# Loading the first x rows of a SiLU layer's forward and backward pass as four 128-row tiles, and starting the first matmuls on 384 rows

## The chip, the cores and the metric

The kernel runs on one core of one Trainium2 chip. The metric is the device time of one execution in microseconds (us), as a median over runs. The profile's span (first to last recorded instruction) is 1.7 to 2.4 us shorter than that time. Moments such as "5.25 us" count from the start of the span. PE is TensorE, PEld its weight loads, DVE VectorE, ACT ScalarE, SP SyncE.

## The reference

```python
B, S, D, F = 1, 2048, 640, 1536          # all bfloat16
def forward(x, w1, w2):
    h = einsum("bsd,df->bsf", x, w1)
    return einsum("bsf,fd->bsd", silu(h), w2)
# outputs: forward(x, w1, w2) and the gradients for x, w1, w2, given grad_out
```

That is six matrix products of 2048 x 640 x 1536.

## The kernel before

The 2048 rows are worked in four chunks of 512. Each chunk needs x transposed (`xT`, D on the partitions). Chunks 1 to 3 use a DMA transpose. Chunk 0 loads x as it lies and transposes it on TensorE, 20 blocks of 128x128. Ahead of that stand 36 matmuls on zeros ("warm-ups"): the first matmuls of this program run at half pace, 107 ns from start to start against 56 ns later (shown below), and the warm-ups are there to take up that time.

```python
warm = cpool.tile([P, P], dt_in, name="warm")
nc.vector.memset(warm[:], 0.0)
...                                            # activation table is loaded here
for i in range(NWARM):                         # NWARM = 36
    nc.tensor.matmul(wp[:, 0:P], lhsT=warm[:], rhs=warm[:], start=True, stop=True)
...
def pe_xT(c, halves):                          # called as pe_xT(0, 1)
    xT = xpool.tile([P, DT, SC], dt_in, name="xT")
    ...
        for dt_ in range(DT):                  # 5 blocks of D
            tp = ps_h.tile([P, nst, P], dt_in, name="tp", tag="hp")
            for j in range(nst):               # 4 blocks of rows
                nc.tensor.transpose(tp[:, j, :], x_nat[:, st, dt_*P:(dt_+1)*P], ident[:])
            ...                                # copy to xT, DVE and ACT in turn
# one queue (SP), in this order: 640 KB of x, two pieces of w1 (320 KB each), the rest
nc.sync.dma_start(out=x_nat[:, 0:STC, :], in_=x_v[:, 0:STC, :])
nc.sync.dma_start(out=w1_nat[:, :, 0:FH], in_=w1_v[:, :, 0:FH])       # FH = 256 columns
nc.sync.dma_start(out=w1_nat[:, :, FH:FC], in_=w1_v[:, :, FH:FC])
...
def h_group(ft, xT, aT, ghT):                  # 12 of these make the h stage of a chunk
    hp = ps_h.tile([P, SC], FP32, name="hp")
    for dt_ in range(DT):
        nc.tensor.matmul(hp[:], lhsT=w1_nat[:, dt_, ft*P:(ft+1)*P], rhs=xT[:, dt_, :],
                         start=(dt_ == 0), stop=(dt_ == DT - 1))
    ...                                        # silu and its derivative on ACT and DVE
```

In chunk 0 the h stage (60 matmuls) is followed by the output stage (60 matmuls with w2). The moment at which the output stage's first matmul starts tells how long the head and the h stage took together.

Of the kernel before, what the change touches and what calls it, by code (L numbers as in the profile page):

```python
# [8 lines left out]
ACT = mybir.ActivationFunctionType  # L9
ALU = mybir.AluOpType  # L10
FP32 = mybir.dt.float32
# [4 lines left out]
def kernel(  # L16
# [11 lines left out]
    nc = tc.nc  # L28
    P = 128
# [8 lines left out]
    ST, DT, FT = S // P, D // P, F // P  # L38
    SC = 512
    NCH = S // SC  # L40
    STC = SC // P
    DH = D // 2
    FC = 512
    NFC = F // FC
    LAG = 2
    NWARM = 36
    dt_in = x.dtype

    dram = ctx.enter_context(tc.tile_pool(name="dram", bufs=1, space=bass.MemoryType.DRAM))
# [2 lines left out]
    ps_h = ctx.enter_context(tc.tile_pool(name="ps_h", bufs=8, space=bass.MemoryType.PSUM))  # L52
# [8 lines left out]
    x_nat = natpool.tile([P, ST, D], dt_in, name="x_nat")  # L61

    w1_v = w1.rearrange("(dt p) f -> p dt f", p=P)
    w2_v = w2.rearrange("(ft p) d -> p ft d", p=P)
    x_v = x2.rearrange("(st p) d -> p st d", p=P)
# [17 lines left out]
    with ExitStack() as mctx:  # L83
        cpool = mctx.enter_context(tc.tile_pool(name="cpool", bufs=1))
        wpool = mctx.enter_context(tc.tile_pool(name="wpool", bufs=1))
        xpool = mctx.enter_context(tc.tile_pool(name="xpool", bufs=2))
# [1 line left out]
        tpool = mctx.enter_context(tc.tile_pool(name="tpool", bufs=3))  # L88
        opool = mctx.enter_context(tc.tile_pool(name="opool", bufs=2))

        warm = cpool.tile([P, P], dt_in, name="warm")
        nc.vector.memset(warm[:], 0.0)  # L92
        warm_a = cpool.tile([P, 1], FP32, name="warm_a")
        nc.scalar.activation(warm_a[:], warm[:, 0:1], ACT.Silu)
        wp = ps_h.tile([P, SC], FP32, name="wp", tag="hp")
        for i in range(NWARM):
            nc.tensor.matmul(wp[:, 0:P], lhsT=warm[:], rhs=warm[:], start=True, stop=True)  # L97

        ident = cpool.tile([P, P], dt_in, name="ident")
        make_identity(nc, ident[:])  # L100

        w1_nat = w1pool.tile([P, DT, F], dt_in, name="w1_nat", tag="w1a")
# [4 lines left out]
        def load_xT(c):  # L107
            xT = xpool.tile([P, DT, SC], dt_in, name="xT")
            nc.sync.dma_start_transpose(out=xT[:], in_=x2[c * SC:(c + 1) * SC, :])
            return xT  # L110

        def load_goT(c):
            goT = xpool.tile([P, DT, SC], dt_in, name="goT")
            nc.sync.dma_start_transpose(out=goT[:], in_=go2[c * SC:(c + 1) * SC, :])
            return goT

        def pe_xT(c, halves):
            xT = xpool.tile([P, DT, SC], dt_in, name="xT")
            nst = STC // halves
            for hh in range(halves):  # L120
                for dt_ in range(DT):
                    tp = ps_h.tile([P, nst, P], dt_in, name="tp", tag="hp")
                    for j in range(nst):
                        st = c * STC + hh * nst + j
                        nc.tensor.transpose(tp[:, j, :], x_nat[:, st, dt_ * P:(dt_ + 1) * P], ident[:])  # L125
                    dst = xT[:, dt_, hh * nst * P:(hh + 1) * nst * P]
                    if dt_ % 2 == 0:
                        nc.vector.tensor_copy(out=dst, in_=tp[:].rearrange("p j q -> p (j q)"))
                    else:
                        nc.scalar.copy(out=dst, in_=tp[:].rearrange("p j q -> p (j q)"))  # L130
            return xT

        FH = FC // 2
        nc.sync.dma_start(out=x_nat[:, 0:STC, :], in_=x_v[:, 0:STC, :])
        nc.sync.dma_start(out=w1_nat[:, :, 0:FH], in_=w1_v[:, :, 0:FH])
        nc.sync.dma_start(out=w1_nat[:, :, FH:FC], in_=w1_v[:, :, FH:FC])
        for fc in range(1, NFC):
            nc.sync.dma_start(out=w1_nat[:, :, fc * FC:(fc + 1) * FC], in_=w1_v[:, :, fc * FC:(fc + 1) * FC])
        for hf in range(2):
            nc.sync.dma_start(out=w2_nat[:, :, hf * DH:(hf + 1) * DH], in_=w2_v[:, :, hf * DH:(hf + 1) * DH])  # L140
        goT_next = load_goT(0)
# [1 line left out]
            nc.sync.dma_start_transpose(out=w2T[:, :, fc * FC:(fc + 1) * FC], in_=w2[fc * FC:(fc + 1) * FC, :])  # L143
        nc.sync.dma_start_transpose(out=w1T[:], in_=w1[:, :])

        xT_next = pe_xT(0, 1)

        def h_group(ft, xT, aT, ghT):
            hp = ps_h.tile([P, SC], FP32, name="hp")
            for dt_ in range(DT):  # L150
                nc.tensor.matmul(  # L151
                    hp[:],
                    lhsT=w1_nat[:, dt_, ft * P:(ft + 1) * P],
                    rhs=xT[:, dt_, :],
                    start=(dt_ == 0),
                    stop=(dt_ == DT - 1),
                )
            nc.scalar.activation(aT[:, ft, :], hp[:], ACT.Silu)  # L158
            t = tpool.tile([P, SC], FP32, name="t")
            nc.scalar.activation(t[:], hp[:], ACT.Tanh, scale=0.5)  # L160
            v = tpool.tile([P, SC], dt_in, name="v")
            nc.vector.tensor_scalar(out=v[:], in0=t[:], scalar1=-0.5, scalar2=0.5, op0=ALU.mult, op1=ALU.add)  # L162
            nc.vector.scalar_tensor_tensor(  # L163
                out=ghT[:, ft, :], in0=aT[:, ft, :], scalar=1.0, in1=v[:], op0=ALU.subtract, op1=ALU.mult
            )

        def g_group(ft, goT, ghT):
            gp = ps_h.tile([P, SC], FP32, name="hp")
            for dt_ in range(DT):
                nc.tensor.matmul(  # L170
                    gp[:],
                    lhsT=w2T[:, dt_, ft * P:(ft + 1) * P],
                    rhs=goT[:, dt_, :],
                    start=(dt_ == 0),
                    stop=(dt_ == DT - 1),
                )
            nc.vector.scalar_tensor_tensor(  # L177
                out=ghT[:, ft, :], in0=ghT[:, ft, :], scalar=1.0, in1=gp[:], op0=ALU.add, op1=ALU.mult
            )
# [21 lines left out]
        for c in range(NCH):  # L201
            xT, goT = xT_next, goT_next
            aT = apool.tile([P, FT, SC], dt_in, name="aT")
            ghT = apool.tile([P, FT, SC], dt_in, name="ghT")

            if c + 1 < NCH:
                xT_next = load_xT(c + 1)
                goT_next = load_goT(c + 1)
            if c == 1:
                for j in range(0, ST, STC):  # L210
                    nc.sync.dma_start(out=go_nat[:, j:j + STC, :], in_=go_v[:, j:j + STC, :])
            if c == 2:
                for j in range(STC, ST, STC):
                    nc.sync.dma_start(out=x_nat[:, j:j + STC, :], in_=x_v[:, j:j + STC, :])

            if c == 0:
                for ft in range(FT):
                    h_group(ft, xT, aT, ghT)
                nc.sync.dma_start(
                    out=aT_scr[:, c * SC:(c + 1) * SC].rearrange("(ft p) s -> p ft s", p=P), in_=aT[:]  # L220
                )
                sd_phase(c, w2_nat, aT, oT_scr)
                for ft in range(FT):
                    g_group(ft, goT, ghT)
                nc.sync.dma_start(
                    out=ghT_scr[:, c * SC:(c + 1) * SC].rearrange("(ft p) s -> p ft s", p=P), in_=ghT[:]
                )
                sd_phase(c, w1T, ghT, gxT_scr)
                continue

            for i in range(FT + LAG):
                if i < FT:
                    h_group(i, xT, aT, ghT)
                if i >= LAG:
                    g_group(i - LAG, goT, ghT)

            store_rows(c - 1, opool)
            nc.sync.dma_start(
                out=aT_scr[:, c * SC:(c + 1) * SC].rearrange("(ft p) s -> p ft s", p=P), in_=aT[:]
            )  # L240
            nc.sync.dma_start(
                out=ghT_scr[:, c * SC:(c + 1) * SC].rearrange("(ft p) s -> p ft s", p=P), in_=ghT[:]
            )
            if c == NCH - 1:
                load_a_blk(0, w1pool, "w1a")

            sd_phase(c, w2_nat, aT, oT_scr)
            sd_phase(c, w1T, ghT, gxT_scr)

    with ExitStack() as fctx:  # L250
# [19 lines left out]
        for fc in range(NFC):  # L270
            a_blk = a_blks[fc]
            g2T = fpool.tile([P, DT, FC], dt_in, name="g2T")
            for dt_ in range(DT):
                gp = ps_h.tile([P, FC], FP32, name="hp")
                for st in range(ST):
                    nc.tensor.matmul(  # L276
                        gp[:],
                        lhsT=go_nat[:, st, dt_ * P:(dt_ + 1) * P],
                        rhs=a_blk[:, st, :],
                        start=(st == 0),  # L280
                        stop=(st == ST - 1),
# [15 lines left out]
        for fc in range(NFC):  # L297
            gh_blk = gh_blks[fc]
            for dt_ in range(DT):
                if dt_ == DT // 2:  # L300
                    store_gw2(fc)
                if fc == NFC - 1 and dt_ == DT - 1:
                    for k, (lo, hi) in enumerate(((0, FC - P), (FC - P, FC))):
                        gp = ps_h.tile([P, FC], FP32, name="hp")
                        for st in range(ST):
                            nc.tensor.matmul(  # L306
                                gp[:, lo:hi],
                                lhsT=x_nat[:, st, dt_ * P:(dt_ + 1) * P],
                                rhs=gh_blk[:, st, lo:hi],
                                start=(st == 0),  # L310
                                stop=(st == ST - 1),
# [4 lines left out]
                        else:  # L316
                            nc.vector.tensor_copy(out=g1[:, lo:hi], in_=gp[:, lo:hi])  # L317
                        nc.sync.dma_start(
                            out=gw1_v[:, dt_, fc * FC + lo:fc * FC + hi], in_=g1[:, lo:hi]
# [3 lines left out]
                for st in range(ST):  # L323
                    nc.tensor.matmul(  # L324
                        gp[:],
                        lhsT=x_nat[:, st, dt_ * P:(dt_ + 1) * P],
                        rhs=gh_blk[:, st, :],
                        start=(st == 0),
                        stop=(st == ST - 1),
# [38 lines left out]
```

## Time and profile before

321.74 us (three runs). The busy table of the page gives this row for TensorE and its weight loads, busy us, share of the span and instructions:

```profile
PE 316.2 (99%) x1512; PEld 146.7 (46%) x1512; DVE 101.9 (32%) x179; ACT 78.3 (24%) x140; POOL 0.7 (0%) x6
```

TensorE bounds the kernel. The chain of waits, in order of time (start us, duration us, what the end waited for), for the first 20 us:

```profile
0.74 4.51 DMA x_nat<-in_x_dram
5.25 0.05 issue
5.30 1.29 PE tp L125 x20
6.59 12.95 PE hp L151 x60
```

The reader is to see a head of 6.6 us, then one stream: 60 matmuls in 12.95 us, 216 ns each, and so on to 317.5 us without a gap. The timeline of TensorE shows the warm-ups, the transposes and h:

```profile
0.99 4.02 PE L97 MATMUL wp<-warm 128*128 128x128 bf16 x36 [0.99 <-DVE warm L92]
5.30 1.29 PE L125 MATMUL tp<-ident,x_nat 128*128 128x128 bf16 x20 [0.28 <-DMA x_nat<-in_x_dram]
```

36 warm-ups start 107 ns apart. The 20 transposes have the same size but take 64 ns each, 56 ns from start to start: between the last warm-up and 5.30 us the clock has been released to full pace. (The clock column of the windows below prints 1.00 throughout and does not show this release; it is read from the spacing of equal instructions.) Windows of half a microsecond show how x arrives. The columns are the window, its length, busy us (and instructions) of PE, PEld, DVE, ACT and POOL, the granted clock, the DMA share and GB/s; only the last two matter here:

```profile
1.75:2.25 0.50, 0.50 (x8) 0.50 (x7) 0.00 (x0) 0.47 (x2) 0.00 (x0) 1.00 0.74 115
2.25:2.75 0.50, 0.50 (x7) 0.50 (x6) 0.00 (x0) 0.00 (x0) 0.00 (x0) 1.00 0.65 125
2.75:3.25 0.50, 0.50 (x8) 0.50 (x6) 0.00 (x0) 0.00 (x0) 0.00 (x0) 1.00 0.83 261
```

### The profile page before, as it was taken

Reading aid. Unit: us, or ns where it says so; the run is one execution under the profiler, and the core shown is the slowest. Engines: PE = TensorE matmul, PEld = TensorE weight load, DVE = VectorE, ACT = ScalarE, POOL = GpSimd, SP = SyncE. Lnnn points to the kernel's source line nnn. Section 1 sums busy time; section 2 is a strip of 40 time slices with the busy share of each in tenths; the row PEclk is TensorE's granted clock in tenths of the full one; section 3 lists DMA queues with packets and bytes.
Section 4 is the critical chain, followed back from the end, with each engine's and each line's share of the span. In section 5 each row is a group of like instructions: output and inputs, shape, how many; then the busy total and the mean of one; then the engine's idle time right before and its main releaser. Section 6 shows DMA issues by size and latency. Waiting matters only on the chain.

```text
span 320.1 us, 3590 instructions
## 1 busy us (share of the span) xinstructions
PE 316.2 (99%) x1512; PEld 146.7 (46%) x1512; DVE 101.9 (32%) x179; ACT 78.3 (24%) x140; POOL 0.7 (0%) x6
## 2 busy tenths in 40 slices
PE   8999999999999999999999999999999999999996
PEld 7444444444444444444444444444444444444443
DVE  1871551477510087710147751000000100001001
ACT  3960001555201255401154520110100001001100
POOL 0000000000000000000000000000000000000000
DMA  8999999999999855291635079809999999994111
GB/s 232 314 194 190 252 222 274 341 263 309 262 286 296 227 180 151 69 324 63 175 109 146 2 247 269 224 16 301 260 241 242 269 209 342 238 293 166 52 37 47
DMA packets 149200, 66.69 MB, mean 208 GB/s; under 512 B 112576, under 2 KB 149184, under 8 KB 149184
## 3 DMA queue, kind: packets, MB, share of 16 engines
q1 hardware_dynamic: 149184, 66.46, 81.8%
q8 instruction: 12, 0.20, 0.3%
q14 instruction: 4, 0.03, 0.0%
HBM read 9.18 MB, written 28.97 MB: 119 GB/s over the span
## 4 chain that ended last, share of the span: by engine, by line
PE 98%; DMA 1%; DVE 0%; issue 0%; DVEq 0%
PE hp L186 32%; PE hp L151 16%; PE hp L276 16%; PE hp L170 16%; PE hp L324 15%; DMA x_nat<-in_x_dram 1%; PE hp L306 1%; PE tp L125 0%; DVE g_2364 L317 0%; DVEq L317 0%
## 5 line engine op out<-in xcount | busy, mean ns | idle before, releaser
L151 PE MATMUL hp<-xT,w_nat 128*128 128x512 bf16 x240 | 56.9, 379 | 0.0
L170 PE MATMUL hp<-goT,w2T 128*128 128x512 bf16 x240 | 56.9, 379 | 0.0
L186 PE MATMUL hp<-aT,w_nat 128*128 128x512 bf16 x240 | 52.5, 379 | 0.0
L186 PE MATMUL hp<-ghT,w1T 128*128 128x512 bf16 x240 | 52.5, 379 | 0.0
L276 PE MATMUL hp<-a_blk,go_nat 128*128 128x512 bf16 x240 | 52.0, 379 | 0.0
L324 PE MATMUL hp<-gh_blk,x_nat 128*128 128x512 bf16 x224 | 48.5, 379 | 0.0
L194 ACT ACTIVATE oT<-hp 128x512 bf16<-128x512 f32 x24 | 14.3, 597 | 110.0 <-PE hp L186 110.0
L186 PEld LDWEIGHTS <-w_nat 128*128 128x128 bf16 x240 | 23.5, 98 | 28.3
L170 PEld LDWEIGHTS <-w2T 128*128 128x128 bf16 x240 | 23.5, 98 | 28.3
L276 PEld LDWEIGHTS <-go_nat 128*128 128x128 bf16 x240 | 23.5, 98 | 28.3
L186 PEld LDWEIGHTS <-w1T 128*128 128x128 bf16 x240 | 23.4, 98 | 28.4
L158 ACT ACTIVATE aT<-hp 128x512 bf16<-128x512 f32 x48 | 28.7, 598 | 31.1 <-PE hp L151 31.1
L151 PEld LDWEIGHTS <-w_nat 128*128 128x128 bf16 x240 | 23.4, 98 | 28.1
L196 DVE CAST oT<-hp 128x512 bf16<-128x512 f32 x16 | 11.1, 692 | 78.0 <-PE hp L186 78.0
L177 DVE SCALAR_TENSOR_TENSOR ghT<-ghT,hp 128x512 bf16<-128x512 bf16 x48 | 32.5, 683 | 7.3 <-PE hp L170 7.3
L324 PEld LDWEIGHTS <-x_nat 128*128 128x128 bf16 x224 | 21.9, 98 | 26.4
L163 DVE SCALAR_TENSOR_TENSOR ghT<-aT,v 128x512 bf16<-128x512 bf16 x48 | 33.0, 688 | 0.6
L162 DVE TENSOR_SCALAR v<-t 128x512 bf16<-128x512 f32 x48 | 20.5, 427 | 28.5 <-ACT t L160 28.5
L160 ACT ACTIVATE t<-hp 128x512 f32<-128x512 f32 x48 | 28.4, 591 | 0.0
L286 DVE CAST g2T<-hp 128x512 bf16<-128x512 f32 x7 | 4.8, 692 | 46.1 <-PE hp L276 46.1
L284 ACT ACTIVATE g2T<-hp 128x512 bf16<-128x512 f32 x8 | 4.8, 598 | 47.0 <-PE hp L276 47.0
L97 PE MATMUL wp<-warm 128*128 128x128 bf16 x36 | 4.0, 313 | 1.0 <-DVE warm L92 1.0
(32 smaller groups left out, 27.0 us busy)
## 6 DMA issues: line engine op xcount, KB each, us to landing
aT_scr<-aT SPq DMA_DIRECT2D x4, 1536.0 KB, 6.2
ghT_scr<-ghT SPq DMA_DIRECT2D x4, 1536.0 KB, 10.1
out_dram<-o_sb SPq DMA_DIRECT2D x8, 640.0 KB, 3.4
x_nat<-in_x_dram SPq DMA_DIRECT2D x4, 640.0 KB, 4.7
oT_scr<-oT SPq DMA_DIRECT2D x4, 640.0 KB, 4.3
go_nat<-in_grad_out_dram SPq DMA_DIRECT2D x4, 640.0 KB, 7.1
gxT_scr<-oT SPq DMA_DIRECT2D x4, 640.0 KB, 4.7
w_nat<-in_w_dram SPq DMA_DIRECT2D x2, 960.0 KB, 11.3
```

What stands on the lines that cost most here:

```text
L151: nc.tensor.matmul(hp[:], lhsT=w1_nat[:, dt_, ft * P:(ft + 1) * P], rhs=xT[:, dt_, :], start=(dt_ == 0), stop=(dt_ == DT - 1),)
L158: nc.scalar.activation(aT[:, ft, :], hp[:], ACT.Silu)
L160: nc.scalar.activation(t[:], hp[:], ACT.Tanh, scale=0.5)
L162: nc.vector.tensor_scalar(out=v[:], in0=t[:], scalar1=-0.5, scalar2=0.5, op0=ALU.mult, op1=ALU.add)
L163: nc.vector.scalar_tensor_tensor(out=ghT[:, ft, :], in0=aT[:, ft, :], scalar=1.0, in1=v[:], op0=ALU.subtract, op1=ALU.mult)
L170: nc.tensor.matmul(gp[:], lhsT=w2T[:, dt_, ft * P:(ft + 1) * P], rhs=goT[:, dt_, :], start=(dt_ == 0), stop=(dt_ == DT - 1),)
L177: nc.vector.scalar_tensor_tensor(out=ghT[:, ft, :], in0=ghT[:, ft, :], scalar=1.0, in1=gp[:], op0=ALU.add, op1=ALU.mult)
L186: nc.tensor.matmul(op_[:], lhsT=w_all[:, ft, dt_ * P:(dt_ + 1) * P], rhs=rhs_all[:, ft, :], start=(ft == 0), stop=(ft == FT - 1),)
L194: nc.scalar.activation(oT[:, dt_, :], op_[:], ACT.Copy)
L196: nc.vector.tensor_copy(out=oT[:, dt_, :], in_=op_[:])
L276: nc.tensor.matmul(gp[:], lhsT=go_nat[:, st, dt_ * P:(dt_ + 1) * P], rhs=a_blk[:, st, :], start=(st == 0), stop=(st == ST - 1),)
L324: nc.tensor.matmul(gp[:], lhsT=x_nat[:, st, dt_ * P:(dt_ + 1) * P], rhs=gh_blk[:, st, :], start=(st == 0), stop=(st == ST - 1),)
```

## The change

The intent is to start h earlier: load x as four tiles of 128 rows on two queues, transpose each as it lands, and run h's first two column groups on the first 384 rows, with tile 3 transposed between them. Warm-ups drop from 36 to 26 and start earlier, on a constant that exists anyway; four filler matmuls cover the last copy.

```diff
-    NWARM = 36
+    NWARM = 26
+    NFILL = 4
-        warm = cpool.tile([P, P], dt_in, name="warm")
-        nc.vector.memset(warm[:], 0.0)
+        warm = nc.const_aps.tensor(1.0, (P, P), dt_in)
 ...
-        nc.sync.dma_start(out=x_nat[:, 0:STC, :], in_=x_v[:, 0:STC, :])
-        nc.sync.dma_start(out=w1_nat[:, :, 0:FH], in_=w1_v[:, :, 0:FH])
-        nc.sync.dma_start(out=w1_nat[:, :, FH:FC], in_=w1_v[:, :, FH:FC])
+        load_x_tile(nc.sync, 0)
+        load_x_tile(nc.scalar, 1)
+        load_x_tile(nc.scalar, 2)
+        load_w1(0, FH)
+        load_x_tile(nc.sync, 3)
+        load_w1(FH, FC)
 ...                                  # the activation table is loaded behind these issues
-        xT_next = pe_xT(0, 1)
+        def pe_x_tile(xT, st):       # 3 blocks -> one DVE copy, 2 blocks -> one ACT copy
+            ...
+        for st in range(STC - 1):
+            pe_x_tile(xT_next, st)
+        for i in range(NFILL):
+            nc.tensor.matmul(wp[:, 0:P], lhsT=ident[:], rhs=x_nat[:, STC-2, 0:P], ...)
 ...
             if c == 0:
-                for ft in range(FT):
+                for ft in range(2):                    # XL = 384
+                    h_mm(hp, ft, xT, 0, XL)
+                    if ft == 0:
+                        pe_x_tile(xT, STC - 1)
+                for ft in range(2):
+                    h_mm(hps[ft], ft, xT, XL, SC)
+                    h_group(ft, xT, aT, ghT, hps[ft])
+                for ft in range(2, FT):
                     h_group(ft, xT, aT, ghT)
```

More of the change, by code (lines that the diff above doesn't have):

```diff
@@ L89 @@
         opool = mctx.enter_context(tc.tile_pool(name="opool", bufs=2))
-        warm = cpool.tile([P, P], dt_in, name="warm")
-        nc.vector.memset(warm[:], 0.0)
+        warm = nc.const_aps.tensor(1.0, (P, P), dt_in)
         warm_a = cpool.tile([P, 1], FP32, name="warm_a")
-        nc.scalar.activation(warm_a[:], warm[:, 0:1], ACT.Silu)
         wp = ps_h.tile([P, SC], FP32, name="wp", tag="hp")
         for i in range(NWARM):
-            nc.tensor.matmul(wp[:, 0:P], lhsT=warm[:], rhs=warm[:], start=True, stop=True)
+            nc.tensor.matmul(wp[:, 0:P], lhsT=warm, rhs=warm, start=True, stop=True)
         ident = cpool.tile([P, P], dt_in, name="ident")
@@ L115, in load_goT, with load_w1, load_x_tile @@
             return goT
-        def pe_xT(c, halves):
-            xT = xpool.tile([P, DT, SC], dt_in, name="xT")
-            nst = STC // halves
-            for hh in range(halves):
-                for dt_ in range(DT):
-                    tp = ps_h.tile([P, nst, P], dt_in, name="tp", tag="hp")
-                    for j in range(nst):
-                        st = c * STC + hh * nst + j
-                        nc.tensor.transpose(tp[:, j, :], x_nat[:, st, dt_ * P:(dt_ + 1) * P], ident[:])
-                    dst = xT[:, dt_, hh * nst * P:(hh + 1) * nst * P]
-                    if dt_ % 2 == 0:
-                        nc.vector.tensor_copy(out=dst, in_=tp[:].rearrange("p j q -> p (j q)"))
-                    else:
-                        nc.scalar.copy(out=dst, in_=tp[:].rearrange("p j q -> p (j q)"))
-            return xT
-        FH = FC // 2
-        nc.sync.dma_start(out=x_nat[:, 0:STC, :], in_=x_v[:, 0:STC, :])
-        nc.sync.dma_start(out=w1_nat[:, :, 0:FH], in_=w1_v[:, :, 0:FH])
-        nc.sync.dma_start(out=w1_nat[:, :, FH:FC], in_=w1_v[:, :, FH:FC])
+        FH = FC // 2
+        XL = SC - P
+        xT_next = xpool.tile([P, DT, SC], dt_in, name="xT")
+        def load_w1(lo, hi):
+            nc.sync.dma_start(out=w1_nat[:, :, lo:hi], in_=w1_v[:, :, lo:hi])
+        def load_x_tile(eng, st):
+            eng.dma_start(out=x_nat[:, st, :], in_=x_v[:, st, :])
+        load_x_tile(nc.sync, 0)
[4 more added lines that the diff above has]
+        load_w1(FH, FC)
         for fc in range(1, NFC):
-            nc.sync.dma_start(out=w1_nat[:, :, fc * FC:(fc + 1) * FC], in_=w1_v[:, :, fc * FC:(fc + 1) * FC])
+            load_w1(fc * FC, (fc + 1) * FC)
+        nc.scalar.activation(warm_a[:], warm[:, 0:1], ACT.Silu)
         for hf in range(2):
@@ L144, with h_mm @@
         nc.sync.dma_start_transpose(out=w1T[:], in_=w1[:, :])
-        xT_next = pe_xT(0, 1)
-        def h_group(ft, xT, aT, ghT):
-            hp = ps_h.tile([P, SC], FP32, name="hp")
+        DS = 3
+        def pe_x_tile(xT, st):
+            for lo, hi, copy in ((0, DS, nc.vector.tensor_copy), (DS, DT, nc.scalar.copy)):
+                tp = ps_h.tile([P, hi - lo, P], dt_in, name="tp", tag="hp")
+                for dt_ in range(lo, hi):
+                    nc.tensor.transpose(tp[:, dt_ - lo, :], x_nat[:, st, dt_ * P:(dt_ + 1) * P], ident[:])
+                copy(out=xT[:, lo:hi, st * P:(st + 1) * P], in_=tp[:])
+        for st in range(STC - 1):
+            pe_x_tile(xT_next, st)
+        for i in range(NFILL):
+            nc.tensor.matmul(
+                wp[:, 0:P], lhsT=ident[:], rhs=x_nat[:, STC - 2, 0:P], start=True, stop=True
+            )
+        def h_mm(hp, ft, xT, lo, hi):
             for dt_ in range(DT):
                 nc.tensor.matmul(
-                    hp[:],
+                    hp[:, lo:hi],
                     lhsT=w1_nat[:, dt_, ft * P:(ft + 1) * P],
-                    rhs=xT[:, dt_, :],
+                    rhs=xT[:, dt_, lo:hi],
                     start=(dt_ == 0),
@@ L157, in h_group @@
                 )
+        def h_group(ft, xT, aT, ghT, hp=None):
+            if hp is None:
+                hp = ps_h.tile([P, SC], FP32, name="hp")
+                h_mm(hp, ft, xT, 0, SC)
             nc.scalar.activation(aT[:, ft, :], hp[:], ACT.Silu)
@@ L216 @@
             if c == 0:
-                for ft in range(FT):
+                hps = []
+                for ft in range(2):
+                    hp = ps_h.tile([P, SC], FP32, name="hp")
+                    h_mm(hp, ft, xT, 0, XL)
+                    hps.append(hp)
+                    if ft == 0:
[4 more added lines that the diff above has]
+                for ft in range(2, FT):
                     h_group(ft, xT, aT, ghT)
```

## The prediction

> **What bounds the kernel now.** The busy table has TensorE busy 316.2 of 320.1 us (99%). The chain of waits is 98% TensorE, one unbroken stream from 5.30 us to nearly the end: 12.95 us for each 60 matmuls, so 216 ns for a 128x512 one. 1440 of them are 311 us. Outside lie only the head and some 2.7 us of tail; the change touches the head alone. There the chain reads: x load 0.74 to 5.25 us (4.51, one 640 KB transfer), 20 transposes 5.30 to 6.59 (64 ns each), then h. The timeline agrees: warm-up matmuls from 0.99 us, 107 ns apart (cold pace), the last started at 4.70, a wait for x, h from 6.42.
>
> **What the change does.**
> - The memset (0.11 us) goes; TensorE starts near 0.75. No gain by itself: data is what is waited for. 26 warm-ups at 107 ns end near 3.5.
> - h waits for three tiles of x (480 KB, not 640) and, as before, 320 KB of w1. By short windows, data flows from 1.75 us, at 100 to 190 GB/s until 3.0, then 330 to 400. With completion some 0.5 us after the last byte I estimate tile 0 near 3.6, tile 1 near 3.8, tile 2 near 4.5, the w1 piece near 5.0. The Trainium skill ("DMA: Bandwidth & Descriptors", section "Issuing engines are not separate DMA queues") says that transfers issued by several engines run on the same 16 DMA engines and save issue time only. The trace before used one issuer and cannot show this; I expect no bandwidth from the second.
> - 10 of 20 transposes (0.64 us) hide under arrival; tile 2's five (0.32) and a copy (estimate 0.4, from 0.42 for a 128x512 DVE copy) stay ahead of h, the four fillers running meanwhile. h starts near 5.4 to 5.6, about 1.0 us earlier.
> - Given back inside the stream: tile 3's five transposes (0.32 us), and two groups as 384+128 columns: ten more small matmuls, about 0.1 us (64 ns against 54 for a quarter). Perhaps 0.1 of waits.
>
> Net about 0.5 to 0.6 us at the end of h. All later work is the same matmul stream, and its weights should be there in time, so the gain is kept. The activation table load moves behind two ACT issues, to about 1.8 to 3.1 us, before its first use near 4: free.
>
> **Prediction.** 321.1 us, 80% range 320.2 to 322.2. Faster by over 2%: 1%; within 2%: 98%; slower by over 2%: 1%.
>
> **What would show it.** The chain's x load ends near 4.5 to 5.0 (or w1 stands in its place); h begins near 5.5; the h stage ends near 19.0 instead of 19.54; later stages keep their length, shifted alike. Fifteen transposes before h, five inside.
>
> **What would make it wrong.**
> - The clock: transposes ran at full pace from 5.3 us, after 3.7 us of unbroken warm-ups. The Trainium skill ("TensorE: Matmul & The Clock Gate", section "The HAM clock gate") says that about 3.4 us of sustained activity, in a free-running window, releases it. Fewer warm-ups and pauses between tiles may delay that; h would begin at half pace (up to 1.7 us lost, an estimate): up to 322.5.
> - w1 is held back by the second queue's tiles, so h waits for weights.
> - Four transfers pay more start-up than one, or two queues fill the slow first microsecond better than I think; then up to 1.2 us is won (320.5).

## More of the kernel before

The closing waits of SyncE (name, count, duration ns min/median/max, first and last start):

```profile
L363 SPq EVENT_SEMAPHORE  x7: 17/28/28, 318.2 to 320.0; - x7
```

and, from two timelines, the output stage's first matmul and the issue of the last store:

```profile
19.38 0.81 PE L186 MATMUL hp<-aT,w_nat 128*128 128x512 bf16 x3
317.84 0.33 SPq L318 DMA_DIRECT2D out_dram<-g_2364  x1
```

## The result, and the profile after

322.11 us (322.0 to 322.3, four runs) against 322.05 us (321.65 to 322.4, four runs). The ratio is 1.0003, 95% interval 0.9986 to 1.002: the same. A ratio here is the mean time of one kernel's fast runs over that of the other's of the same rounds, so it is not quite the ratio of the medians quoted. The time lies inside the predicted range, at its upper end, but the gain of about 0.6 us is not there.

The busy row and the chain of waits after, for the same 20 us:

```profile
PE 314.6 (98%) x1487; PEld 146.9 (46%) x1516; DVE 101.8 (32%) x179; ACT 77.9 (24%) x142; POOL 0.7 (0%) x6
...
1.16 4.07 DMA x_nat<-in_x_dram
5.23 0.04 issue
5.28 0.35 PE tp L148 x3
5.63 0.02 issue
5.65 0.37 DVE xT L149
6.02 0.04 issue
6.07 0.97 PE hp L160 x5
7.04 0.28 PE tp L148 x5
```

(The busy row is lower only because some matmul records are missing in this trace.) Tile 2 landed at 5.23 us, no earlier than all of x before (5.25). h starts at 6.07 instead of 6.42, 0.35 us earlier. Tile 3's transposes (0.28 us) stand inside the stream. The output stage's first matmul starts at 19.32 us, before at 19.38: the head's gain is 0.06 us.

```profile
19.32 1.03 PE L200 MATMUL hp<-aT,w_nat 128*128 128x512 bf16 x3
317.78 0.33 SPq L342 DMA_DIRECT2D out_dram<-g_2375  x1
```

The windows answer to those before:

```profile
1.75:2.25 0.50, 0.50 (x8) 0.50 (x6) 0.00 (x0) 0.50 (x1) 0.00 (x0) 1.00 0.82 161
2.25:2.75 0.50, 0.50 (x7) 0.50 (x6) 0.00 (x0) 0.50 (x1) 0.00 (x0) 1.00 0.87 230
2.75:3.25 0.50, 0.50 (x7) 0.50 (x6) 0.00 (x0) 0.40 (x2) 0.00 (x0) 1.00 0.94 322
```

Data flows faster at the start than before. Then the closing waits:

```profile
L387 SPq EVENT_SEMAPHORE  x7: 17/28/1087, 318.2 to 320.2; - x7
```

One wait of 1087 ns stands where before none was over 28 ns. The last store is issued 0.06 us earlier (317.78 against 317.84 us), yet the span is longer (320.3 against 320.1): from that issue to the end 2.52 us pass, before 2.27.

So there are two questions: why does the head gain so little, and where does the longer tail come from? My first theory for the head (A) was that tile 2 is late because it shares the DMA engines with the w1 piece on the other queue; the rival (B) was a fixed cost for each small transfer.

### The profile page after: what moved, and what is told of

Its sections match the earlier page's. It is cut to its first block, busy times and chain, and to the rows that moved or that the text cites. A ratio compares the mean times of both kernels' runs of the same rounds, so it can differ in the third digit from the quotient of the medians.

```text
span 320.3 us, 3575 instructions
## 1 busy us (share of the span) xinstructions
PE 314.6 (98%) x1487; PEld 146.9 (46%) x1516; DVE 101.8 (32%) x179; ACT 77.9 (24%) x142; POOL 0.7 (0%) x6
## 4 chain that ended last, share of the span: by engine, by line
PE 97%; DMA 1%; issue 1%; DVE 0%; ACTq 0%; DVEq 0%
PE hp L200 32%; PE hp L184 16%; PE hp L160 16%; PE hp L300 16%; PE hp L348 15%; DMA x_nat<-in_x_dram 1%; PE hp L330 1%; PE tp L148 0%; ACTq L124 0%; DVE xT L149 0%; DVE g_2375 L341 0%; DVEq L341 0%
## 5 line engine op out<-in xcount | busy, mean ns | idle before, releaser
L160 PE MATMUL hp<-xT,w_nat 128*128 128x512 bf16 (+2 forms) x243 | 56.7, 370 | 0.5
```

The costliest lines, as they stand in the source:

```text
L160: nc.tensor.matmul(hp[:, lo:hi], lhsT=w1_nat[:, dt_, ft * P:(ft + 1) * P], rhs=xT[:, dt_, lo:hi], start=(dt_ == 0), stop=(dt_ == DT - 1),)
```

## The experiments

Moments in this table are us from the span's start. "Landed" is the sixteenth (last) increment of the transfer's semaphore in the trace; "released" is between the last pair of 128-column weight loads that start 107 ns apart and the first that start 56 ns apart (a single moment is approximate, where other work lies between them); "output" is the output stage's first matmul; "tail" is from the issue of the last store to the end.

| trace | tile 2 landed | w1 piece landed | released | h starts | output | tail | span |
|---|---|---|---|---|---|---|---|
| before | 5.25 (all x) | 6.36 | 4.7 to 5.3 | 6.42 | 19.38 | 2.27 | 320.1 |
| e7, before again | 5.06 (all x) | 6.14 | 6.8 to 7.0 | 7.09 | 20.04 | 2.28 | 320.8 |
| e10, before + 3 transfers | 5.13 (all x) | 6.25 | 3.8 to 3.9 | 6.30 | 19.26 | 2.52 | 320.2 |
| after | 5.23 | 5.36 | 4.4 to 5.3 | 6.07 | 19.32 | 2.52 | 320.3 |
| e6, after again | 4.14 | 5.10 | 4.8 to 4.9 | 5.66 | 18.91 | 2.51 | 319.9 |
| e11, after, third | 4.10 | 5.45 | about 4.0 | 5.49 | 18.76 | 2.52 | 319.7 |
| e9, after + 5 transfers | 5.26 | 5.25 | 5.4 to 5.6 | 6.21 | 19.45 | 2.27 | 320.2 |
| e8, no fillers | 4.24 | 5.23 | about 6.6 | 5.87 | 19.48 | 2.52 | 320.5 |
| e12, 10 warm-ups | 4.02 | 5.07 | about 7.8 | 5.63 | 19.95 | 2.51 | 320.9 |
| e1, tile 2 first | 3.94 | 6.10 | about 4.3 | 6.15 | 19.41 | 2.55 | 320.4 |
| e2, one queue | 4.91 | 6.24 | about 3.4 | 6.28 | 19.84 | 2.54 | 320.8 |
| e3, w1 behind tile 3 | 4.54 | 6.27 | about 6.7 | 6.32 | 19.77 | 2.52 | 320.8 |
| e4, no split | 4.32 | 5.20 | 3.2 to 3.9 | 6.59 | 19.54 | 2.52 | 320.5 |
| e5, w1 on ACT | 5.35 | 4.51 | 3.8 to 5.0 | 6.19 | 19.44 | 2.51 | 320.4 |

The trace files also hold the throttle's own record of the clock, which no view prints as moments; it was read from them (trace.npz). Its stretch of full clock begins at 3.40 us in e2, 3.86 in e4, 3.93 in e10, 4.01 in e11, 4.32 in e1, 4.90 in the trace after, 4.93 in e6, 4.98 in e5, 5.56 in e9, 6.64 in e8, 6.75 in e3, 6.93 in e7 and 7.83 in e12; the first trace of the kernel before has no such record. Each stretch lasts 314.03 or 317.44 us, which is 92 or 93 times 3.413 us.

All kernels were correct.

### e1: tile 2 ahead of the w1 piece

```diff
         load_x_tile(nc.sync, 0)
         load_x_tile(nc.scalar, 1)
-        load_x_tile(nc.scalar, 2)
+        load_x_tile(nc.sync, 2)
         load_w1(0, FH)
         load_x_tile(nc.sync, 3)
```

> The changed kernel with one edit: x tile 2 goes on the SP queue right behind tile 0, ahead of the first w1 piece (tile 1 alone stays on the ACT queue). Theory A (tile 2 lands late, at 5.24 us, because it shares the DMA engines with the w1 piece queued on the other queue): tile 2's transposes start near 4.5 us instead of 5.28, the first h matmul near 5.3 to 5.5 instead of 6.07 (then bound by the w1 piece), the output stage starts near 18.6 to 18.8 instead of 19.32. Rival B (small transfers and a second queue cost a fixed time each, whatever the order): tile 2's transposes still start at or after 5.0, the output stage within 0.15 us of 19.32. Time: A 321.5, B 322.1.

Measured: 322.24 us, ratio 0.9999 (0.9982 to 1.0015). Tile 2 lands at 3.94 as theory A wants, but h starts no earlier: the w1 piece now lands at 6.10 instead of 5.36. TensorE's weight loads wait for it:

```profile
3.67 1.13 PEld L148 LDWEIGHTS <-x_nat 128*128 128x128 bf16 x15 [0.23 <-DMA x_nat<-in_x_dram]
4.76 0.27 PEld L154 LDWEIGHTS <-ident 128*128 128x128 bf16 x4
6.14 0.60 PEld L160 LDWEIGHTS <-w_nat 128*128 128x128 bf16 x5 [1.12 <-DMA w_nat<-in_w_dram]
```

And the windows of e1 show why it came so late. After a good start the rate falls to half while the SP queue begins the w1 piece and the ACT queue is empty:

```profile
2.75:3.25 0.50, 0.50 (x7) 0.50 (x6) 0.00 (x0) 0.00 (x0) 0.00 (x0) 1.00 1.08 372
3.25:3.75 0.50, 0.50 (x6) 0.27 (x4) 0.00 (x0) 0.00 (x0) 0.00 (x0) 1.00 0.65 217
3.75:4.25 0.50, 0.50 (x6) 0.50 (x7) 0.04 (x1) 0.00 (x0) 0.00 (x0) 1.00 0.71 170
```

So A and B both miss. h needs three tiles and the w1 piece, 800 KB; bringing one part forward put the other back.

### e2: all tiles on the SP queue

```diff
-        load_x_tile(nc.scalar, 1)
-        load_x_tile(nc.scalar, 2)
+        load_x_tile(nc.sync, 1)
+        load_x_tile(nc.sync, 2)
```

> The changed kernel with all four x tiles on the SP queue in the order 0, 1, 2, w1 piece, 3; nothing on the ACT queue. Theory A (order decides): tile 2's transposes start near 4.5 us, about as with tile 2 first on two queues, h near 5.4. If the second queue itself speeds up the slow first microsecond (in the trace after, about 270 KB had arrived by 3.0 us against about 165 KB before), tile 0 lands no earlier than 3.6 here and tile 2 some 0.2 to 0.3 us later than with two queues. Rival B (fixed cost for each transfer): tile 2 at 5.0 or later. Second question, the tail: from the issue of the last store to the end the kernel before took 2.26 us and the changed one 2.5; if use of the ACT queue costs this, the tail here is 2.25, otherwise it stays 2.5 or varies freely.

Measured: 322.6 us, ratio 1.0009 (0.9994 to 1.0024). Tile 0 landed at 3.06, earlier than with two queues (3.36 to 3.81 in the seven traces with the change's loads), and tile 1 at 3.42, about as there (3.38 to 3.79). Two of its windows:

```profile
2.25:2.75 0.50, 0.50 (x7) 0.50 (x6) 0.00 (x0) 0.00 (x0) 0.00 (x0) 1.00 0.99 320
3.25:3.75 0.50, 0.50 (x11) 0.50 (x9) 0.00 (x0) 0.00 (x0) 0.00 (x0) 1.00 0.75 156
```

From 2.25 to 2.75 us one queue moved 320 GB/s, where one 640 KB transfer had moved 125 (110 and 164 in e7 and e10). The fast start thus comes from the small transfers and not from the second queue; my expectation of a slower start missed. Tile 2 landed at 4.91 (thirteen of its sixteen increments by 4.2, the other three from 4.7 on), the w1 piece at 6.24, with the same hole in the rate as in e1 (156 and 141 GB/s from 3.25 to 4.25 us). The second w1 piece came at 8.99 and held h up again, so the output stage starts at 19.84. The tail is 2.54 without any use of the ACT queue: that queue is not its cause.

### e3: the w1 piece behind tile 3

```diff
-        load_w1(0, FH)
         load_x_tile(nc.sync, 3)
+        load_w1(0, FH)
```

> The changed kernel with the first w1 piece issued after tile 3 on the SP queue; tiles 1 and 2 stay on the ACT queue. Only tile 3 (160 KB) now runs beside tile 2, not 320 KB of w1. Theory A: tile 2's transposes start 0.4 to 0.8 us earlier than 5.28 (near 4.6 to 4.9), although its queue and its size are unchanged; h then waits for w1 instead and starts near 5.6 to 5.8. Rival B (the second transfer of the ACT queue is slow by itself): still 5.2 or later.

Measured, one look: tile 2 landed at 4.54 and the w1 piece at 6.27; h at 6.32, a quarter microsecond worse. The run looked like support for A. It is not: e6 and e11, below, show tile 2 at 4.1 with no edit at all. What stands is that, with x in tiles, a w1 piece issued later on the SP queue lands later: issued at 1.2 us it lands at 5.1 to 5.5 (seven traces), at 1.7 at 6.10 and 6.27, at 2.1 at 6.24. The moment of issue alone does not set it: the later ones also have more x ahead of them on their queue, and in the kernel before, issued at 1.2 to 1.3 us behind all 640 KB of x, the piece lands at 6.14 to 6.36. In this trace the clock was also released late: the transposes start 107 ns apart, and h's first group takes 1.18 us instead of 0.97.

### e4: the loads of the change, without the split

```diff
-        for st in range(STC - 1):
+        for st in range(STC):
             pe_x_tile(xT_next, st)
 ...
-                # ft 0 and 1 on 384 rows, tile 3 between them, then the last 128
+                for ft in range(FT):
+                    h_group(ft, xT, aT, ghT)
```

> The changed kernel's loads and warm-ups, but h waits for all four tiles: 20 transposes ahead of h, no 384+128 split. It shows what the split alone buys. Tile 3's last packet came at 5.27 us in the trace after, so it should land near 5.8; transposes 5.8 to 6.15, copy, h near 6.5. With 60 full matmuls of 216 ns after that and nothing given back the output stage starts near 19.4: about the 19.38 of the kernel before and within 0.15 us of the changed kernel's 19.32. If instead the split is worth its intended half microsecond, it starts near 19.8.

Measured, one look: tile 3 landed at 5.66, h at 6.59, output at 19.54. Against the first trace after (19.32) the split buys 0.22 us; against e6 and e11, in which tile 2 landed early as it did here, it buys 0.6 to 0.8. The intended half microsecond of the split exists.

### e5: the w1 piece first, on the ACT queue

```diff
         load_x_tile(nc.sync, 0)
-        load_x_tile(nc.scalar, 1)
-        load_x_tile(nc.scalar, 2)
-        load_w1(0, FH)
+        load_w1(0, FH, nc.scalar)
+        load_x_tile(nc.sync, 1)
+        load_x_tile(nc.sync, 2)
         load_x_tile(nc.sync, 3)
```

> The changed kernel with the queues swapped: the first w1 piece alone on the ACT queue (issued first, at 0.74 us), the four x tiles in order on the SP queue, the other w1 pieces behind them. Theory C (h starts when the last of three x tiles and the w1 piece, 800 KB together, has landed, and what moves that moment is how early the 640 descriptors of the w1 piece are issued and whether both queues stay fed; issued at 1.19 it landed at 5.36, issued at 1.67 at 6.10, at 2.12 at 6.24): issued at 0.74 it lands near 4.9 to 5.3; tile 2 near 4.6 to 4.9; h starts near 5.3 to 5.5, the output stage near 18.6 to 18.8 (19.32 after, 19.38 before), the median 321.5. Rival D (the bytes set it: 800 KB cannot be there before about 5.3 and something else always takes its place): h not before 5.9, output stage within 0.2 us of 19.32, time unchanged.

Measured: 322.24 us, ratio 1.0013 (0.9999 to 1.0027). The w1 piece landed at 4.51, early as hoped, but tile 1 at 4.91 and tile 2 at 5.35. The last of the 800 KB came at 5.35, as in the changed kernel (5.36, 5.10, 5.45), and h started later than in e6 because behind the last tile still stand transposes and a copy (0.84 us from landing to h), behind the w1 piece nothing (0.04 us in e11). The rival D is nearer: I found no order that had all 800 KB there before 5.0 us. The order can only choose what comes last, and of the orders tried w1 last was best.

### e6 and e11: the changed kernel again

> The changed kernel once more, unedited, with five rounds against the kernel before: for a narrower interval and a second trace of the head. If the first trace is typical, tile 2 lands at 5.1 to 5.4, h starts at 6.0 to 6.2 and the output stage at 19.2 to 19.5; ratio 0.999 to 1.001. If the first trace was a lucky or an unlucky one, h starts more than 0.3 us away from 6.07.

> The changed kernel, unedited, a third trace and the reference for the other runs of this call. Theory R (release of the clock at a moment that varies from run to run, 3.4 to 6.9 us in the traces so far): output stage at 18.9 if the release comes before about 5 us, 19.4 to 19.6 if it comes after 6, and against the kernel before at a like release (19.38 early, 20.04 late) 0.4 to 0.5 us earlier. Tail 2.5. If instead the head gain is nil at equal release, it starts at 19.3 or later with an early release.

Measured: e6 322.27 us (321.67 to 324.35), ratio 1.0031 (1.0006 to 1.0056); e11 322.34 us (321.6 to 324.23), ratio 1.0039 (1.0016 to 1.0062). The chain of e11:

```profile
1.20 4.24 DMA w_nat<-in_w_dram
5.45 0.05 issue
5.49 0.99 PE hp L160 x5
6.48 0.28 PE tp L148 x5
```

The first trace was not typical. Tile 2 landed at 4.0 to 4.3 in five of the seven traces with these loads (e4, e6, e8, e11, e12), and at 5.2 to 5.3 in two (after, e9). The packet records of the trace files show what goes with it. In the two traces with a late tile 2 the SP queue's first packet starts before the ACT queue's (1.76 against 1.96 us, and 1.77 against 1.90), and the first packet of the w1 piece at 2.87 and 2.72. In the other five the ACT queue's is first (1.75 to 1.76, SP 1.92 to 2.18), and the w1 piece begins at 3.08 to 3.37. So there is a race between the two queues, and in all seven traces the queue that starts first also goes on first with its second transfer (tile 2 on ACT, the w1 piece on SP). The first issues of the two queues lie within 6 ns in each of them; what decides the race is not shown, and no run forced it. With tile 2 early, h starts at 5.49 and 5.66 us and the output stage at 18.76 and 18.91, where the kernel before, with the clock released before x lands, has 19.38 and 19.26 (e10, whose head is the same). The means differ by 0.48 us: here the predicted gain of 0.5 to 0.6 us at the end of h is nearly present. The best spans are nevertheless alike, 319.7 after and 319.8 before. Both of these traces are of the fastest of their six runs. The ordinary spans between 320.2 and 320.6 have only one trace, the first one, with a late tile 2; whether that is what holds the others there is not shown.

The repeated rounds showed something else: of all 16 spans of the unedited changed kernel, 12 lie at 319.7 to 320.6 (mean 320.28) and four at 322.3 to 322.6. Of 29 spans of the kernel before in the rounds of the experiments, none is above 320.8 (mean 320.18). The four slow ones are under the 1.5% at which a run counts as slow, so the ratios above include them.

### e7: the kernel before again

No edit.

> The kernel before, unedited, for a second trace. In its first one the time from the issue of the last store to the end was 2.27 us, in all five others 2.52 to 2.55; and its times fall in two groups, near 321.7 and near 322.5. If the short tail was chance, this run has 2.5; if the kernel before has it always, 2.27. The head: the first w1 piece landed at 6.36 and h started at 6.42; expected again within 0.2 us, unless the release of the clock comes later than 5.3 us, in which case the 20 transposes run at half pace and h starts up to 1 us later: this would be the slower group.

Measured, one look: 322.56 us, of unknown state. The tail is 2.28, so it is a property of the kernel. The timeline of TensorE in e7:

```profile
0.98 4.02 PE L97 MATMUL wp<-warm 128*128 128x128 bf16 x36 [0.98 <-DVE warm L92]
5.11 2.14 PE L125 MATMUL tp<-ident,x_nat 128*128 128x128 bf16 x20
7.09 7.29 PE L151 MATMUL hp<-xT,w_nat 128*128 128x512 bf16 x32
```

x landed 0.19 us earlier than in the first trace, but the 20 transposes take 2.14 us instead of 1.29: the clock was released only at 6.8 to 7.0. The output stage starts 0.66 us later, and the span is 320.8 instead of 320.1. So the moment of release alone moves the same kernel by about as much as the change was meant to gain. This would account for the two groups of its times, near 321.7 and 322.5, but it rests on one trace of each release.

### e8: no fillers

```diff
-    NFILL = 4
+    NFILL = 0
```

> The changed kernel without its four filler matmuls. If they only use time in which TensorE waits for the copy of tile 2, nothing moves: h at 6.0 to 6.2, output stage within 0.15 us of 19.32. If they keep the clock released, h runs at half pace for up to 3 us here and the output stage starts up to 1.5 us later.

Measured, one look: h at 5.87, output at 19.48. The clock was released at about 6.6, and h's first weight loads start 270 and 320 ns apart (162 ns at full pace). That is the second expected outcome in form, but late release occurs with fillers too (e3) and in the kernel before (e7), and here TensorE paused for under half a microsecond. One trace cannot tell; what the fillers do stays open.

### e9 and e10: the tail

At the end SyncE waits in a fixed order for the semaphores that transfers use, which are handed out in turn. In the kernel before (88 transfers) the last store's semaphore comes last in that order. The change has 91 transfers, the last store gets a semaphore that is waited for first, and four more waits, 62 to 66 ns apart, follow its landing. e9 adds five transfers to the changed kernel, e10 adds three to the kernel before, in both by cutting the loads of grad_out in the second chunk:

```diff
-                for j in range(0, ST, STC):
-                    nc.sync.dma_start(out=go_nat[:, j:j + STC, :], in_=go_v[:, j:j + STC, :])
+                for j, n in ((0, 2), (2, 2), (4, 2), (6, 2), (8, 2), (10, 2), (12, 2), (14, 1), (15, 1)):
+                    nc.sync.dma_start(out=go_nat[:, j:j + n, :], in_=go_v[:, j:j + n, :])
 # e10, on the kernel before: ((0, 2), (2, 2), (4, 2), (6, 2), (8, 2), (10, 2), (12, 4))
```

> The changed kernel with the four loads of the grad_out rows (in the second chunk, far from the critical path) cut into nine: five more transfers. Reason: in all traces of the kernel before, SyncE's closing waits end on the last store's semaphore, and 2.27 us pass from that store's issue to the end; with the three more transfers of the changed kernel the last store falls on a semaphore that is waited for first, four more waits follow its landing, and the tail is 2.48 to 2.55. With eight more than before the last store is back on the semaphore waited for last. Theory T (the order of the closing waits): the tail is 2.25 to 2.30, and the median is 0.2 to 0.25 us below that of the changed kernel in the same rounds. Rival (the tail belongs to something else in the change): 2.48 to 2.55 again.

> The reverse: the kernel before with the same four loads cut into seven, three more transfers and nothing else. Theory T: the tail grows from 2.27 to 2.5 us and the median is 0.2 to 0.25 us above the kernel before, with an unchanged head. Rival: tail 2.27. The trace also gives a third head of the kernel before: with the clock released before x lands (5.1 to 5.3) the output stage starts at 19.2 to 19.4; released later, up to 20.1, because the 20 transposes and then h run at half pace.

The closing waits, first of e9:

```profile
L387 SPq EVENT_SEMAPHORE  x7: 17/28/28, 318.3 to 320.1; - x7
```

and of e10:

```profile
L363 SPq EVENT_SEMAPHORE  x7: 17/28/1093, 318.1 to 320.2; - x7
```

The tail is 2.27 in e9 and 2.52 in e10 (in every other trace with a long tail it is 2.51 to 2.55; the 2.48 of the expectation was a slip): the wait of over a microsecond goes and comes with the count alone. Theory T is shown, by both directions. In time: e9 321.99 us, 0.35 below the changed kernel of the same rounds (322.34), but one long run in e9 and two in e11 make that difference. Without them the mean spans are 320.22 and 320.28, so the times do not show the quarter microsecond; the tails of the traces do. e10 322.34 us against 321.70, ratio 1.002 (1.0008 to 1.0032), somewhat more than the tail's 0.25 us explains.

### e12: 10 warm-ups

```diff
-    NWARM = 26
+    NWARM = 10
```

> The changed kernel with 10 warm-up matmuls instead of 26: TensorE pauses from about 1.9 us to the arrival of tile 0 near 3.7. If the release needs unbroken activity (as the prediction feared for 26 warm-ups), it comes at 5.5 us or later in the profile, most of h's first groups run at half pace, and spans rise by 0.3 to 1 us over those of the changed kernel in the same rounds. If only the phase of the window matters, spans stay at those of the changed kernel within 0.15 us.

Measured: 323.74 us, ratio 1.0058 (1.0040 to 1.0076). The weight loads of TensorE in the timeline:

```profile
0.74 0.99 PEld L96 LDWEIGHTS <-const-bfloat16-1.0 128*128 128x128 bf16 x10 [0.74 <-issue]
3.61 1.52 PEld L148 LDWEIGHTS <-x_nat 128*128 128x128 bf16 x15 [1.87 <-DMA x_nat<-in_x_dram]
...
6.58 0.15 PEld L160 LDWEIGHTS <-w_nat 128*128 128x128 bf16 x1 [0.17 <-issue]
6.89 0.15 PEld L148 LDWEIGHTS <-x_nat 128*128 128x128 bf16 x1 [0.17 <-issue]
7.21 0.47 PEld L148 LDWEIGHTS <-x_nat 128*128 128x128 bf16 x4 [0.17 <-issue]
7.64 1.45 PEld L160 LDWEIGHTS <-w_nat 128*128 128x128 bf16 x14
```

A single weight load every 320 ns is h's 384-column matmuls at half pace; the clock is released at about 7.8 us, later than in any other trace. All data was there early (h starts at 5.63), yet the output stage starts at 19.95. The six spans are 320.9 to 323.0, all above the 12 ordinary ones of the changed kernel. A pause of 1.9 us in the warm-ups thus costs one microsecond and more: the release does depend on activity, not on the window's phase alone.

## Why the prediction was right or wrong

- Luck: that the time lies in the range. Predicted was 321.1 us, 0.64 below the 321.74 then known; measured was 322.11, 0.06 above 322.05. The range reached up to 322.2 and so held a result without any gain; the later medians of the same kernel, 322.27 and 322.34, lie outside it.
- Right: TensorE bounds the kernel, only the head is at stake, and the rest of the stream keeps its length. From the output stage's start to the issue of the last store 298.46 us pass in both kernels (317.84 - 19.38 and 317.78 - 19.32).
- Right, if a little less than predicted: what is given back inside the stream. Predicted were 0.4 us and perhaps 0.1 of waits. From h's first matmul to the output stage 12.95 us pass before and 13.25 after, 0.30 us more.
- Right in five of seven traces, wrong in the first: "tile 2 near 4.5". It lands at 4.0 to 4.3 or at 5.2 to 5.3, and in the profiled run that was quoted it was the latter, with the SP queue's packets first; this is the term that failed there ("h starts near 5.4 to 5.6": 6.07). Where tile 2 is early and the clock released early, h starts at 5.49 to 5.66 and the h stage ends 0.48 us earlier, a little less than predicted.
- Wrong: "so the gain is kept". Some 0.25 us of it is lost at the other end of the program. Three more transfers moved the last store to a semaphore that the closing waits take first; e9 and e10 show it. I had counted the transfers' cost at the start only.
- The named risk was real, and it is not peculiar to the change: the kernel before has it too (e7). I read one trace of the kernel before and took "full pace from 5.3 us" as its state. The Trainium skill ("TensorE: Matmul & The Clock Gate", section "The HAM clock gate") speaks of a free-running window and some 3.4 us of activity; the traces agree: stretches of full clock last a whole number of 3.413 us, and their beginning is not fixed. It lies between 3.4 and 6.9 us in the traces with 26 or 36 warm-ups, and at 7.8 with 10. Work that the change moves forward into half pace gains only half: in e8 (release near 6.6) the output stage starts at 19.48, 0.6 us later than in e6 and e11. But e8's 19.48 stands against e7's 20.04, so at late release too the changed head seems to be ahead; it is one trace of each, and e8's release is 0.3 us earlier.
- Argued, not shown: four of 16 runs of the changed kernel at 322.3 to 322.6 us, 2.0 us above the rest, would fit a release that comes one whole window of 3.4 us later (half of that is lost, 1.7 us, an estimate with the window of that page). The kernel before, whose 36 warm-ups run unbroken to 5.0 us, has no such run in 29, and with fewer warm-ups (e12) long spans are more frequent. No trace caught one, so a late w1 piece cannot be excluded as their cause.
- Right, and for a reason I had half wrong: "no bandwidth from the second" queue. The Trainium skill ("DMA: Bandwidth & Descriptors", section "Issuing engines are not separate DMA queues") says so, and e2 agrees: one queue with small transfers moved 320 GB/s from 2.25 to 2.75 us, two queues 230 in the first trace and 292 to 347 in the six others with the same loads. But four transfers paid less start-up than one (110 to 164 GB/s in three traces), where I feared more.

The sum, then: about 0.5 us won in the head when tile 2 is early, 0.06 in the trace first taken; 0.25 us lost at the tail; and some runs, four of 16, that are 2 us longer for a cause that no trace caught. The measured ratio was 1.0003 at first and 1.0031 and 1.0039 later. No version that I ran beats the kernel before; e9, with the tail repaired, has 1.0018 (0.9998 to 1.0038).

## What to carry to other kernels

When a change is worth a fraction of a microsecond, take several traces of each kernel before reading a cause from one: here the clock's release and the landing of one 160 KB tile each moved by more than the change was worth. Ask of everything the first matmul needs when the last of it lands, and let that last thing be one that needs no further step. Adding or removing transfers can move the end of the program by a quarter of a microsecond through the order of the closing waits, so look at the tail even when only the head was touched.

## What the Trainium skill lacked or had wrong

- "TensorE: Matmul & The Clock Gate", section "The HAM clock gate": it gives the release at about 4 us into sustained activity, plus or minus 500 ns from run to run. With warm-ups unbroken from 0.99 to 4.5 us or later it came at 3.9 us in e10 and at 6.9 in e7, which have the same head, so 2.9 to 6.0 us after the first matmul; in e2 it was 2.6 us. The same page advises not to fit to a count; the spread here is worth 0.7 us of span.
- The same section, activity: a 1.9 us pause between 10 warm-ups and the first real work put the release at about 7.8 us and raised the spans to 320.9 to 323.0, from mostly 319.7 to 320.6. How busy TensorE must be within the window is not stated, and these runs do not settle it.
- "DMA: Bandwidth & Descriptors", section "Bandwidth": its rule is to batch transfers to 1 MiB or more, for the share of peak. It does not tell of the start of a program: one 640 KB load moved 115 and then 125 GB/s in the windows from 1.75 to 2.75 us (108 and 110 in e7, 69 and 164 in e10), 160 KB loads of the same rows 177 and then 320 GB/s on the same single queue (e2). By the landing little of that was left: three tiles, 480 KB, were there at 4.91 us in e2, one load of all 640 KB at 5.06 to 5.25.
- The same page has no word on a hole in the rate behind the first small transfers: 372 GB/s fell to 217 and 170 (e1), 307 to 156 and 141 (e2), and with work on both queues 347 to 190 (e9, from 2.25 to 3.25 us). The turn of a queue from 1280-byte rows of x to 512-byte rows of w1 is not enough for it: the kernel before makes that turn on its only queue and went from 383 to 352 and 338 GB/s (3.75 to 5.25 us). Cause not found.
- No page that I found tells of the closing waits: a last store on the semaphore that is waited for first costs 0.25 us (tail 2.52 against 2.27 us), in the kernel before as in the changed one.
